# Shorter GpSimd subtractions, more filler products and one moved multiplication in a cluster-attention and mixture-of-experts kernel

## The chip, the core and the metric

The kernel runs on one NeuronCore of a Trainium2 chip, in one launch. Its time is device microseconds. Five engines work side by side, each through its own queue in order: TensorE (PE; its weight loads are listed as PEld), VectorE (DVE), ScalarE (ACT), GpSimd (POOL) and SyncE (SP), which issues most of the DMA transfers.

## The reference

Attention over 16 heads (2 batches of 8), 768 positions, 64 dimensions, is masked by cluster: a query sees a key only where both are nearest to the same of 16 centroids. The result goes through a top-1 mixture of 8 experts with a capacity of 384 rows.

```python
q_assign = argmax(einsum('bhsd,hcd->bhsc', q_n, c_n)); k_assign = ...   # per head
scores = where(q_assign == k_assign, q @ k.T / sqrt(D), -1e9)
attn = softmax(scores);  x = (attn @ v)            # (1536, 512) over all heads
expert_idx = argmax(x @ w_gate); gate_w = its softmax probability
disp[e, pos] = x[i] for the first `capacity` rows of each expert
out[i] = gate_w[i] * (relu(disp[e] @ w1[e]) @ w2[e])[pos]
```

All inputs are fp32.

## The kernel before

**Two-part numbers.** A product on TensorE is made of a rounded high part and the remainder, so that fp32 accuracy is kept. ACT makes the high part by a copy to the fp32r type, and DVE or GpSimd makes the remainder by a subtraction. `split` (line 271) does so for q and k of a head in four steps: step 0 copies q into `W` on ACT and subtracts into `ql` on GpSimd (line 284), step 1 copies k into `Y1` on ACT (line 287), step 2 issues two DMAs, step 3 subtracts into `Y0` on GpSimd (line 293). Each subtraction covers 64 partitions by 768 elements and is followed by a DMA on SP that duplicates a part of it. `split_v` (line 165) does it for v of two heads (128 x 780, line 170), and `p_low` (line 372) for the exponentials of two key tiles (128 x 768, line 376), on DVE except for the eight pairs named in `POOL_PL`, which go to GpSimd.

**A head.** `max_tile` (line 299) multiplies a key block into a 128 x 384 PSUM tile `m`, and DVE takes the row maximum (line 313). The maxima of a head are turned into a row of `Qs`, so that `st_group` (line 354) gets scores with the maximum subtracted: two products (lines 361 and 362), then two exponentials on ACT (line 370). `pv_group` (line 378) multiplies with v in three products (line 387), the third of which needs the remainder `pl`. The loop over 16 heads `i` and 12 groups `g` runs the score products four groups ahead of the value products, and the maxima half a head to a head ahead. `hooks` (line 554) puts the other work at fixed (i, g): the splits of head i+3, the cluster assignment of the pair after next (`cl_scores` line 176, `cl_assign` line 204, `cl_back` line 255), the output (`out_stage`, line 397), and in head 8 the gate, which ends with six scatters by GpSimd (line 527).

**Order.** The prologue is under `tc.manual_schedule()`: each engine's order there is as written. From `warm()` on the Tile framework's planner orders the instructions by its own costs, between `no_sync_barrier` marks before heads 1 and 3 to 8.

**Fillers.** `keep_warm(n, d)` (line 835) issues n products of a constant 128 x 128 tile whose result nobody reads; each shows as two matmul instructions in the trace. In the prologue, `max_tile` is called with `warm=WARM1` (one filler) for four of its six tiles, and `max_part` issues six.

**After the heads** the experts run (`moe`, line 618), TensorE products throughout, with weight loads, ACT copies and DVE subtractions; GpSimd only scatters rows there.

Of the kernel before, what the change touches and what calls it, by code (L numbers as in the profile page):

```python
# [7 lines left out]
F32 = mybir.dt.float32  # L8
# [4 lines left out]
ALU = mybir.AluOpType  # L13
# [3 lines left out]
P = 128  # L17
# [6 lines left out]
def kernel(  # L24
# [140 lines left out]
    def split_v(pi):  # L165
        v = vt[pi]
        hi = work.tile([P, 2, NT, VW + 1], R32, tag="vh", name="vh", bufs=2)
        lo = work.tile([P, 2, NT, VW + 1], R32, tag="vl", name="vl", bufs=2)
        nc.scalar.activation(out=hi[:, :, :, 0:VW], in_=v, func=AF.Copy)
        nc.gpsimd.tensor_tensor(out=lo[:, :, :, 0:VW], in0=v, in1=hi[:, :, :, 0:VW].bitcast(F32), op=ALU.subtract)  # L170
        vt[pi, "h"], vt[pi, "l"] = hi, lo


# [94 lines left out]

    ql = {}

    def split(h, step, eng=nc.gpsimd):
        par = h % 2
        d = pair[h // 2]
        W, Y1, Qs, Y0 = (pick(t, h) for t in (W_t, Y1_t, Qs_t, Y0_t))
        a, c = MAIN[par], PIECE[par]
        p0, p1 = slice(a.start, a.start + 32), slice(a.start + 32, a.stop)

        def dup(dst, src):
            nc.sync.dma_start(out=dst.bitcast(F32), in_=src.bitcast(F32))

        if step == 0:
            nc.scalar.activation(out=W[a], in_=d["q"][a], func=AF.Copy)  # L282
            ql[h] = work.tile([P, S], R32, tag="ql", name="ql", bufs=2)
            eng.tensor_tensor(out=ql[h][a], in0=d["q"][a], in1=W[a].bitcast(F32), op=ALU.subtract)  # L284
            dup(W[c], ql[h][p0])
        elif step == 1:
            nc.scalar.activation(out=Y1[a], in_=d["k"][a], func=AF.Copy)
            dup(Y1[c], Y1[p0])
        elif step == 2:
            dup(Qs[a], W[a])  # L290
            dup(Qs[c], ql.pop(h)[p1])
        elif step == 3:
            nc.gpsimd.tensor_tensor(out=Y0[a], in0=d["k"][a], in1=Y1[a].bitcast(F32), op=ALU.subtract)
            dup(Y0[c], Y1[p1])


# [75 lines left out]
    def p_low(h, g):  # L372
        if g % 2 == 1:
            ph, pl, pf = pt[h, g]
            eng = nc.gpsimd if (h, g) in POOL_PL else nc.vector
            eng.tensor_tensor(out=pl, in0=pf, in1=ph.bitcast(F32), op=ALU.subtract)  # L376

    def pv_group(h, g):
        j, kt = divmod(g, NT)
# [174 lines left out]
    def hooks(i, g):  # L554
        if g in (3, 9) and 2 <= i < 6:
            zero_fill(2 * (i - 2) + g // 6)
        if i == H and g == 5:
            gens["g"] = gate(0)
        if i == H and g >= 5:
            next(gens["g"], None)  # L560
        if i == 3 and g == 0:
            for c in range(4):
                w_load(c)
        if (i, g) in W_AT:
            c = W_AT.index((i, g))
            w_split(c)
            w_load(c + NA)
        if i == 0:
            if g < 4:
                next(gens["c"], None)  # L570
            if g == 4:
                cl_back(1)
            if g in (2, 3, 4, 5):
                split(2, g - 2)

        n = i + 1
        if g == G_CHAIN and n < NH:
            max_chain(n)
        if g == G_ROWS and n < NH:
            max_rows(n)  # L580
        for st in range(4):
            if i + 3 < NH and g == G_SPLIT[st]:
                split(i + 3, st)
        if (i, g) == (H + 1, 1):
            close_tile()
        if (i, g) == (H + 1, 3):
            row0.append(wra.tile([P, XR], F32, tag="z", name="row0", bufs=1))
            nc.sync.dma_start(out=row0[0], in_=xd[0:P, :])
        if (i, g) == (NH - 1, NT + 4):
            out_stage(i, 0, TH)  # L590
        if (i, g) == (NH - 1, NT + 5):
            gens["g"] = gate(B - 1, 0, TH)
            next(gens["g"], None)
        if i >= 1 and g == G_OUT:
            out_stage(i - 1)
        if i % 2 == 1:
            pi = (i + 1) // 2 + 1
            if pi < NH // 2:
                if g in G_SC:
                    n_ = NT // len(G_SC)  # L600
                    cl_scores(pi, 1, G_SC.index(g) * n_, (G_SC.index(g) + 1) * n_)
                if g == G_AS[0]:
                    gens["c"] = cl_assign(pi, AS_MUL)
                for _ in range(G_AS.count(g)):
                    next(gens["c"], None)
            if g == 0 and (i + 1) // 2 + 2 < NH // 2:
                load_pair((i + 1) // 2 + 2)
            if g == 0 and pi < NH // 2:
                load_v(pi)
        else:  # L610
            pi = i // 2
            if g == G_BACK and i > 0 and pi + 1 < NH // 2:
                cl_back(pi + 1)
            if g == G_SV and pi + 1 < NH // 2:
                split_v(pi + 1)
# [258 lines left out]
    def prologue():  # L874
        nc.vector.memset(onef, 1.0)
        nc.vector.memset(nbig, -BIG)
        nc.sync.dma_start(out=cbr, in_=cb)
        load_pair(0, ("q",))
        nc.sync.dma_start(out=cs, in_=cst)
        load_pair(0, ("k",))  # L880
        load_pair(1)
        load_v(0)
        nc.sync.dma_start(out=rhb, in_=rh)
        load_v(1)
        nc.scalar.activation(out=nbig2, in_=onef[:, 0:1], func=AF.Sqrt)
        keep_warm(5, psM.tile([P, 512], F32, tag="m", name="warm"))
        for lst in (W_t, Y1_t, Qs_t, Y0_t):
            zero_rows(lst, 0)
        one_row(0, 0)
        one_row(1, 0)  # L890
        nc.gpsimd.tensor_copy(c16b, cs[:, C_C16:C_C16 + 16])
        for lst in (W_t, Y1_t, Qs_t, Y0_t):
            zero_rows(lst, 1)
        nc.vector.memset(ohb, 0.0)
        nc.vector.memset(oneb, 1.0)

        sq, fps = centroid_scale()
        cl_scores0("q", 0, 3)
        nf = centroid_spread(sq, fps)
        cl_scores0("q", 3, NT)  # L900
        nc.vector.tensor_copy(idb, ident)
        nc.vector.tensor_tensor(out=cbs, in0=cbr, in1=nf, op=ALU.mult)
        aq, ak = (cl_assign(0, nc.vector, nf[:, 0:1], nm) for nm in "qk")
        next(aq)
        split(0, 0, nc.vector)
        cl_scores0("k")
        split(0, 1)
        nc.scalar.activation(out=nbig2, in_=onef[:, 0:1], func=AF.Exp)
        for _ in aq:
            pass  # L910
        for _ in ak:
            pass

        held = work.tile([P, 1], BF16, tag="held", name="held", bufs=1)
        nc.gpsimd.tensor_copy(held, ohb[:, NT - 1, 96:97])
        cl_scores(1, 3, 0, NT // 2)
        tq = psO.tile([64, S], BF16, tag="o", name="ctq")
        tk = psO.tile([64, S], BF16, tag="o", name="ctk")
        cl_back0("q", tq)
        mask0("q", tq, 0, slice(0, S), nc.scalar)  # L920
        cl_scores(1, 3, NT // 2, NT // 2 + 1)
        split(0, 2)
        cl_back0("k", tk)
        mask0("k", tk, 0, slice(0, HALF), nc.vector)
        mask0("k", tk, 0, slice(HALF, S), nc.scalar)
        split(0, 3)
        mask0("q", tq, 1, slice(0, S), nc.scalar)
        mask0("k", tk, 1, slice(0, S), nc.scalar)
        split(1, 0)
        split(1, 1)  # L930
        split(1, 3)
        split(1, 2)
        split_v(0)
        for j in range(2):
            one_row(j, 1)
        for k in range(NT):
            if k in (1, 3):
                t = NT // 2 + 1 + k // 2
                cl_scores(1, 3, t, t + 1)
            max_tile(0, k // 2, k % 2, *((psS, "s") if k % 5 < 3 else (psM, "m")), warm=0 if k in (1, 3) else WARM1)  # L940
        max_part(0, 0)
        gens["c"] = cl_assign(1, nc.vector)
# [13 lines left out]
    with ExitStack():  # L956
        todo = []
        for i in range(NH):
            if i in (1, 3, 4, 5, 6, 7, 8):
                tc.no_sync_barrier()  # L960
            for g in range(2 * NT):
                st_group(i, g)
                todo.append((i, g))
                if i == 0 and g < NT:
                    max_tile(1, g, 0)
                    max_tile(1, g, 1)
                else:
                    n, k = (i + 1, NT + g) if g < NT else (i + 2, g - NT)
                    if n < NH:
                        max_tile(n, k // 2, k % 2)  # L970
                if len(todo) > PLAG:
                    p_low(*todo[-1 - PLAG])
                if len(todo) > LAG:
                    pv_group(*todo.pop(0))
                hooks(i, g)
# [79 lines left out]
```

## Time and profile before

| | |
|---|---|
| median of 3 runs | 515.59 us (511.2 to 516.54) |
| profiled execution | 517.28 us, span of the trace 515.5 us |
| PE, PEld busy | 486.8 us (94%), 420.4 us (82%) |
| DVE busy | 374.7 us (73%) |
| ACT, POOL busy | 318.2 us (62%), 148.1 us (29%) |
| mean granted TensorE clock | 0.976 of full speed |
| chain that ended last | issue 11%, DMA of weights 2%, the rest below 1% each |

The busy time of PE is an upper bound, since pipelined matmuls overlap in the records. The granted clock is given as a share of 2.4 GHz: 1.00 is 2.4 GHz, and 0.50 is 1.2 GHz. Times of rows count from the start of the span. A bracket at the end of a row says how long the engine had been idle before the instruction and what released it.

### The profile page before, as it was taken

The page shows a single profiled execution, that of the slowest core. Times are in us where ns is not written, and L with a number is a line of the kernel's source. Part 1 is how long each engine was busy: PE and PEld are TensorE (multiplying, and loading weights), DVE is VectorE, ACT ScalarE, POOL GpSimd, SP SyncE. Part 2 cuts the span into 40 slices and gives each one's busy share as a digit, 9 for nine tenths or more (in the row PEclk, how much of TensorE's full clock was granted, in tenths as well). Part 3 has the DMA queues.
Part 4 walks back from the last instruction along what each step waited for, and adds up shares of the span by engine and source line. Part 5 has one row for each costly group of instructions (what it writes and reads, how often), then busy time and mean ns, then how long its engine had stood idle before and what let it go on. Part 6 is the DMA issues. An engine that isn't in the chain of part 4 may idle for free. (4 is left out here: it accounts for less than half of the span.)

```text
span 515.5 us, 8317 instructions
## 1 busy us (share of the span) xinstructions
PE 486.8 (94%) x2917; PEld 420.4 (82%) x2917; DVE 374.7 (73%) x650; ACT 318.2 (62%) x642; POOL 148.1 (29%) x122
## 2 busy tenths in 40 slices
PE   8789999989999997899999999999999999999994
PEld 7667988879889886788888866889898989898873
DVE  5796597987997889999988675584757565665411
ACT  3665497687786986878787853464645445373310
POOL 5677144464434545435100040001000000101001
PEclk9888698999999999999999999999999999999999
DMA  7456436777242453431201038676758484855001
GB/s 227 90 135 186 156 81 242 274 238 237 93 116 69 93 197 89 103 89 33 71 2 42 1 125 314 222 252 203 242 205 287 171 294 149 286 170 197 0 9 41
DMA packets 31152, 77.69 MB, mean 151 GB/s; under 512 B 4710, under 2 KB 5056, under 8 KB 31106
## 3 DMA queue, kind: packets, MB, share of 16 engines
q1 hardware_dynamic: 26162, 60.94, 38.6%
q0 software_dynamic: 4944, 16.15, 8.3%
q8 instruction: 27, 0.44, 0.3%
q14 instruction: 19, 0.16, 0.1%
HBM read 50.07 MB, written 17.45 MB: 131 GB/s over the span
## 5 line engine op out<-in xcount | busy, mean ns | idle before, releaser
L370 ACT ACTIVATE pf<-s 128x384 f32<-128x384 f32 x192 | 94.7, 493 | 58.0 <-PE s L362 46.5
L313 DVE TENSOR_REDUCE mx<-m 128x1 f32<-128x384 f32 x192 | 101.6, 547 | 23.6 <-PE m L306 22.2
L376 DVE TENSOR_TENSOR pl<-pf,ph 128x768 fp32r<-128x768 f32 x88 | 100.2, 1138 | 10.7 <-ACT ph L370 8.3
L132 DVE TENSOR_TENSOR ws<-wraw,ws 128x1024 fp32r<-128x1024 f32 x64 | 78.7, 1248 | 26.5 <-ACT ws L126 26.3
L370 ACT ACTIVATE ph<-s 128x384 fp32r<-128x384 f32 x192 | 94.3, 491 | 0.0
L742 PE MATMUL g<-xh,ws 128*128 128x256 f32 x448 | 80.6, 282 | 0.1
L126 ACT ACTIVATE ws<-wraw 128x1024 fp32r<-128x1024 f32 x64 | 66.0, 1052 | 20.8 <-DMA wraw<-in_w_dram 19.6
L674 PE MATMUL g<-ws,hh 128*128 128x512 f32 x240 | 76.5, 400 | 1.6 <-PEq L831 0.7
L306 PE MATMUL m<-Y,W 112*128 112x384 f32 (+1 forms) x192 | 69.7, 370 | 6.9 <-DVE mx L313 6.3
L387 PE MATMUL o<-pl,vh 128*65 128x384 f32 x192 | 66.8, 348 | 5.2 <-DVE pl L376 4.6
L742 PEld LDWEIGHTS g<-xh,ws 128*128 128x128 f32 x448 | 69.6, 190 | 1.1 <-DVE hl L747 0.3
L527 POOL DMA_INDIRECT out_dram<-y,row x17 | 16.5, 972 | 187.3 <-DVE y L667 135.9
L361 PE MATMUL s<-W,Y 112*128 112x384 f32 (+1 forms) x192 | 69.8, 364 | 0.0
L362 PE MATMUL s<-Qs,Y 97*128 97x384 f32 (+1 forms) x192 | 66.3, 350 | 1.1 <-DMA Qs<-mr 1.0
L387 PE MATMUL o<-ph,vh 128*65 128x384 f32 x192 | 66.2, 345 | 0.0
L387 PE MATMUL o<-ph,vl 128*65 128x384 f32 x192 | 66.1, 344 | 0.0
L742 PE MATMUL g<-xl,ws 128*128 128x256 f32 x224 | 63.1, 282 | 0.0
L746 ACT ACTIVATE hh<-g 128x256 fp32r<-128x256 f32 x56 | 21.4, 385 | 60.6 <-PE g L742 58.7
L674 PEld LDWEIGHTS g<-ws,hh 128*128 128x128 f32 x240 | 43.5, 188 | 11.5 <-issue 1.9
L306 PEld LDWEIGHTS m<-Y,W 112*128 112x128 f32 (+1 forms) x192 | 37.9, 198 | 16.2 <-DVE mx L313 14.7
L674 PE MATMUL g<-ws,hl 128*128 128x512 f32 x120 | 47.3, 394 | 0.3 <-DVE hl L647 0.3
L284 POOL TENSOR_TENSOR ql<-qv,W 64x768 fp32r<-64x768 f32 x15 | 29.2, 1947 | 49.3 <-ACT W L282 32.8
(184 smaller groups left out, 779.6 us busy)
## 6 DMA issues: line engine op xcount, KB each, us to landing
wraw<-in_w_dram SPq DMA_DIRECT2D x64, 512.0 KB
row<-xd SPq DMA_DIRECT2D x25, 260.0 KB
xd<-z POOLq DMA_DIRECT2D x7, 780.0 KB, 5.1
v<-in_v_dram SPq DMA_DIRECT2D x8, 390.0 KB
qv<-in_qT_dram SPq DMA_DIRECT2D x8, 384.0 KB
kv<-in_kT_dram SPq DMA_DIRECT2D x8, 384.0 KB
Y<-Y SPq DMA_DIRECT2D x32, 96.0 KB
Qs<-W SPq DMA_DIRECT2D x16, 192.0 KB
```

Source lines behind the costliest of these rows:

```text
L126: nc.scalar.activation(out=w[:, 0], in_=raw[c], func=AF.Copy)
L132: nc.vector.tensor_tensor(out=w[:, 1], in0=t, in1=w[:, 0].bitcast(F32), op=ALU.subtract)
L284: eng.tensor_tensor(out=ql[h][a], in0=d["q"][a], in1=W[a].bitcast(F32), op=ALU.subtract)
L306: nc.tensor.matmul(out=m[:, 0:HALF], lhsT=W[0:KA[h % 2], t * P:(t + 1) * P], rhs=Y1[0:KA[h % 2], j * HALF:(j + 1) * HALF], start=True, sto ...
L313: nc.vector.tensor_reduce(out=mxt[h][:, j, t:t + 1], in_=m[:, 0:HALF], axis=AX.X, op=ALU.max)
L361: nc.tensor.matmul(out=s[:, 0:HALF], lhsT=Y1[0:ka, ks], rhs=W[0:ka, qs], start=True, stop=False)
L362: nc.tensor.matmul(out=s[:, 0:HALF], lhsT=Y0[0:kb, ks], rhs=Qs[0:kb, qs], start=False, stop=True)
L370: nc.scalar.activation(out=o[:, g % 2], in_=s[:, 0:HALF], func=AF.Exp, scale=1.0 / float(D) ** 0.5)
L376: eng.tensor_tensor(out=pl, in0=pf, in1=ph.bitcast(F32), op=ALU.subtract)
L387: nc.tensor.matmul(out=ot[h, j][0:VW, 0:HALF], lhsT=lhs, rhs=r, start=(kt == 0 and n == 0), stop=(kt == NT - 1 and n == 2))
L674: nc.tensor.matmul(out=ps[:, 0:DM], lhsT=h[:, f, ts], rhs=w[:, a, fs], start=(f == 0 and n == 0), stop=(f == KF - 1 and n == 2),)
L742: nc.tensor.matmul(out=ps[:, 0:w_], lhsT=w[:, a, fs], rhs=x[e][:, k, :], start=(n == 0), stop=(n == 3 * KD - 1))
```

## The change

Four edits. The subtractions on GpSimd are issued in pieces: `ql` and `Y0` in thirds of 256 columns, v and the GpSimd share of `pl` in halves. Where the engine is DVE the instruction stays whole. The cluster code multiplication of the pair assigned in head 9 (`i == H + 1`) goes from GpSimd to DVE. In the prologue four filler products are put before the transposes of the k assignment and two behind them. In head 0 the first of the two maximum tiles of each of the groups 0 to 5 gets one filler product ahead of it.

```diff
-        nc.gpsimd.tensor_tensor(out=lo[:, :, :, 0:VW], in0=v, in1=hi[:, :, :, 0:VW].bitcast(F32), op=ALU.subtract)
+        for j in range(2):
+            nc.gpsimd.tensor_tensor(
+                out=lo[:, j, :, 0:VW], in0=v[:, j], in1=hi[:, j, :, 0:VW].bitcast(F32), op=ALU.subtract
+            )
...
+    def minus(eng, out, a, b):
+        n = out.shape[-1]
+        w = n if eng is nc.vector else -(-n // 3)
+        for c in range(0, n, w):
+            cc = slice(c, min(c + w, n))
+            eng.tensor_tensor(out=out[:, cc], in0=a[:, cc], in1=b[:, cc].bitcast(F32), op=ALU.subtract)
...
-            eng.tensor_tensor(out=ql[h][a], in0=d["q"][a], in1=W[a].bitcast(F32), op=ALU.subtract)
+            minus(eng, ql[h][a], d["q"][a], W[a])
...
-            nc.gpsimd.tensor_tensor(out=Y0[a], in0=d["k"][a], in1=Y1[a].bitcast(F32), op=ALU.subtract)
+            minus(nc.gpsimd, Y0[a], d["k"][a], Y1[a])
...
-            eng.tensor_tensor(out=pl, in0=pf, in1=ph.bitcast(F32), op=ALU.subtract)
+            if eng is nc.vector:
+                eng.tensor_tensor(out=pl, in0=pf, in1=ph.bitcast(F32), op=ALU.subtract)
+            else:
+                for j in range(2):
+                    eng.tensor_tensor(out=pl[:, j], in0=pf[:, j], in1=ph[:, j].bitcast(F32), op=ALU.subtract)
...
-                    gens["c"] = cl_assign(pi, AS_MUL)
+                    gens["c"] = cl_assign(pi, nc.vector if i == H + 1 else AS_MUL)
...
         split(0, 2)
+        keep_warm(4, psM.tile([P, 512], F32, tag="m", name="warm"))
         cl_back0("k", tk)
+        keep_warm(2, psM.tile([P, 512], F32, tag="m", name="warm"))
...
                 if i == 0 and g < NT:
-                    max_tile(1, g, 0)
+                    max_tile(1, g, 0, warm=WARM1)
                     max_tile(1, g, 1)
```

## Rows read from the trace of the kernel before

**Rows 1.** Waits of PE, 60 to 290 us: us in total, times, longest.

```profile
PE m L306 <- DVE mx L313: 4.4, 9, 1.3
PE o L387 <- DVE pl L376: 3.0, 1, 3.0
```

**Rows 2.** Windows: three stretches with the TensorE clock at half.

```profile
15.79:19.20 3.41, 3.41 (x17) 3.41 (x16) 2.04 (x4) 3.35 (x5) 1.01 (x2) 0.50 0.03 5
...
46.51:60.16 13.65, 13.65 (x53) 12.45 (x52) 7.93 (x9) 4.85 (x11) 3.48 (x4) 0.50 0.67 224
77.23:80.64 3.41, 3.41 (x12) 2.85 (x11) 3.27 (x8) 1.74 (x4) 2.42 (x2) 0.50 0.22 68
```

**Rows 3.** Groups of DVE instructions by form: busy us, mean ns, idle before.

```profile
L376 DVE TENSOR_TENSOR pl<-pf,ph 128x768 fp32r<-128x768 f32 x88 | 100.2, 1138 | 10.7 <-ACT ph L370 8.3 <-PE o L387 1.9
...
L425 DVE TENSOR_TENSOR lg<-lg,lt 128x48 f32<-128x48 f32 x13 | 9.6, 737 | 0.0
```

**Rows 4.** Timeline of DVE, prologue and head 0: start us, duration us.

```profile
15.84 0.56 DVE L313 TENSOR_REDUCE mx<-m 128x1 f32<-128x384 f32 x1 [0.55 <-PE m L306]
...
20.54 1.69 DVE L326 TENSOR_TENSOR mxp<-mx 128x3 f32<-128x3 f32 x1
...
22.40 1.62 DVE L503 CAST ebr<-cs 1x8 bf16<-1x8 f32 x1
...
29.19 0.20 DVE L326 TENSOR_TENSOR mxp<-mx 128x3 f32<-128x3 f32 x1
```

**Rows 5.** Timeline of POOL, same stretch.

```profile
20.40 1.80 POOL L293 TENSOR_TENSOR Y<-kv,Y 64x768 fp32r<-64x768 f32 x1
22.28 1.72 POOL L170 TENSOR_TENSOR vl<-v,vh 128x780 fp32r<-128x780 f32 x1
...
29.33 3.91 POOL L293 TENSOR_TENSOR Y<-kv,Y 64x768 fp32r<-64x768 f32 x2
```

**Rows 6.** Timeline of PE, same stretch.

```profile
14.17 0.52 PE L243 MATMUL ctk<-idb,ohb 128*64 128x128 bf16 x6 [0.98 <-DVE ohb L233]
...
19.68 1.50 PE L838 MATMUL mtd<-onef 128*128 128x128 f32 x12
22.28 0.49 PE L332 MATMUL mtd<-cs,mxp 128*1 128x128 f32 x3 [1.09 <-DVE mxp L326]
...
25.00 0.44 PE L306 MATMUL m<-Y,W 112*128 112x384 f32 x1 [1.21 <-DVE mx L313]
```

**Rows 7.** Timeline of DVE: subtractions, and one multiplication, beside GpSimd's or alone.

```profile
31.21 0.35 DVE L225 TENSOR_TENSOR ceq<-ceq,c16b 128x384 bf16<-128x384 bf16 x1
...
38.70 0.94 DVE L376 TENSOR_TENSOR pl<-pf,ph 128x768 fp32r<-128x768 f32 x1
...
46.10 3.22 DVE L376 TENSOR_TENSOR pl<-pf,ph 128x768 fp32r<-128x768 f32 x1
...
70.03 1.80 DVE L376 TENSOR_TENSOR pl<-pf,ph 128x768 fp32r<-128x768 f32 x1
...
194.43 3.91 DVE L376 TENSOR_TENSOR pl<-pf,ph 128x768 fp32r<-128x768 f32 x1
```

**Rows 8.** Timeline of POOL in heads 1 and 9.

```profile
69.16 1.85 POOL L284 TENSOR_TENSOR ql<-qv,W 64x768 fp32r<-64x768 f32 x1 [2.41 <-PE s L361]
70.97 2.56 POOL L293 TENSOR_TENSOR Y<-kv,Y 64x768 fp32r<-64x768 f32 x1
...
193.89 1.87 POOL L284 TENSOR_TENSOR ql<-qv,W 64x768 fp32r<-64x768 f32 x1
195.68 1.83 POOL L293 TENSOR_TENSOR Y<-kv,Y 64x768 fp32r<-64x768 f32 x1
```

**Rows 9.** Timeline of ACT: the copies that the two `Y0` subtractions wait for.

```profile
69.95 0.84 ACT L287 ACTIVATE Y<-kv 64x768 fp32r<-64x768 f32 x1
...
188.08 0.83 ACT L287 ACTIVATE Y<-kv 64x768 fp32r<-64x768 f32 x1
```

**Rows 10.** Waits of SP's own DMA queue: us in total, times, longest.

```profile
SPq L347 <- ACT mr L346: 54.6, 7, 12.7
```

## The prediction

> **What bounds the kernel now.** I read the page first: TensorE is busy nearly throughout and has the largest sum, so time is won where it stands idle or runs slowly. The waits of PE come second. From 60 to 290 us, where the heads run, almost all of its idle time ends at DVE: 4.4 us in 9 waits for a maximum, and 3.0 us in one wait for a subtraction [rows 1]. Third, the windows: the granted clock is 0.50, which is 1.2 GHz instead of 2.4, in stretches of 3.41, 13.65 and 3.41 us [rows 2]; each begins just after a time in which PE had stood idle or done little. At half speed a stretch in which PE is always busy costs up to half its length.
>
> Fourth, why DVE is late. The groups by form show it: the subtraction of 128x768 has a mean of 1138 ns over 88, but one with GpSimd idle takes 0.94 us, so 88 x 0.198 = 17.4 us go in excess; the addition of 48 elements a row has a mean of 737 ns over 13 [rows 3, 7]. The timelines of DVE and POOL, laid side by side, give the cause. A maximum of two 128x3 pieces takes 0.20 us alone and 1.69 us when it starts at 20.54, and it ends at 22.23, where GpSimd's subtraction of 20.40 ends (22.20); a cast of eight elements takes 1.62 us and ends at 24.02, with GpSimd's of 22.28 (24.00) [rows 4, 5]. So a DVE instruction that reads two tiles from SBUF, or casts there, stands until GpSimd's running subtraction is over. The row maxima, which read PSUM, are not slowed.
>
> **The parts and their cost.** The sum is made against the profiled execution's own 517.28 us (a span of 515.5 and 1.8 around it); the median shown, 515.59, is 1.7 lower.
>
> *Pieces: what they cost GpSimd.* ql and Y0 of 15 and 16 heads become thirds, v of 8 pairs and 8 pl become halves: 30 + 32 + 8 + 8 = 78 more instructions. Between neighbours the trace has +0.08 us (20.40 + 1.80 against 22.28) [rows 5] to -0.04 us (69.16 + 1.85 against 70.97) [rows 8], so -3 to +6 us of GpSimd's time in all, at most 0.16 for one split. Its cover is that GpSimd works for a head up to three later. What is queued behind it is on SP: the duplicate of ql waits for GpSimd, and behind that stands the DMA that carries the maxima to the scores. But SP stands 54.6 us waiting for ACT to hand it that row [rows 10], so 0.16 us drowns, and so does one DVE instruction of 0.94 that slips in between pieces. I take 0; with the cover gone it is 0.16 a head, 2.6.
>
> *Pieces: does DVE get in?* In head 1 it did, between ql and Y0: the subtraction that starts at 70.03 took 1.80, while Y0 took 2.56 instead of 1.83 [rows 7, 8]. At 31.21 a multiplication of two SBUF tiles took 0.35 in the middle of two Y0 that follow each other from 29.33 to 33.24 [rows 5, 7]. In head 9 it did not: the one of 194.43 waited through ql and Y0, 3.91 us [rows 7, 8], and one of 3.22 at 46.10 looks alike [rows 7]. I take the first, by the row at 31.21, where GpSimd's second instruction had nothing left to wait for, as a second piece has. The Trainium skill, GPSIMD Engine Reference, "Instruction dispatch", speaks for the other: each of GpSimd's cores begins the next instruction as soon as its own share of the last is done, so that no end of a piece would be free. By the rows taken the sum is 509.0, by that rule it is the first rival's 515.6.
>
> *Pieces: what they give.* If DVE gets in, a wait that now averages half an instruction becomes half of a third or of a half, and GpSimd's cluster multiplications stay whole; I take 40% as what is left. Of PE's 4.4 us of waits for maxima between 60 and 290 [rows 1] that saves 60%, 2.6 (0 to 4.4).
>
> *Head 9.* After the scatters GpSimd does ql and Y0 back to back from 193.89 to 197.5, and DVE's subtraction of 194.43 takes 3.91 instead of 0.94 [rows 7, 8]; that is PE's wait of 3.0 us [rows 1]. A third of 1.87 is 0.62, so DVE starts at 194.5 or 195.1 and ends by 196.1. Of 3.0 I count 2.5 (0 to 3.0).
>
> *The moved multiplication.* GpSimd's queue loses it behind ql and Y0 of head 9, with nothing urgent in line behind it. DVE gains one of 0.35, the time of the same form at 31.21 [rows 7]. It sits among tiles whose result is needed a head later: 0 (-0.35 to +0.35).
>
> *Prologue.* PE waits 0.98 us for the k assignment before its transposes [rows 6]. Twelve filler instructions take 1.50 us, 0.125 each, and a product is two, so four products fill 1.0 us of that and the two behind the transposes 0.5 us, of which about half lies in a wait for the mask. Cost 0 to 0.3. What they aim at is the stretch from 15.79 at half clock [rows 2]. If it stays at 1.00, the six maxima run at DVE's pace, six times 0.56 from 15.84 [rows 4], and end near 19.2 instead of 20.5: 1.3 earlier at most, I take 1.0. Then the small maximum waits for a piece of 0.6 at most, 0.3 in the mean, where it lost 1.69 - 0.20 = 1.49 [rows 4]; PE's transposes waited for it (1.09 idle) [rows 6]. Together 1.0 + 1.2, less the overrun: 2.0 (-0.3 to 2.8).
>
> *Head 0.* The cast of 22.40 would wait for half of 1.72, so it ends some 0.7 earlier [rows 4, 5]; DVE's next maximum ended a wait of PE of 1.21 us [rows 6]. I count 0.7. The six fillers cost 6 x 0.25 = 1.5 us of PE. DVE takes 0.56 us for a maximum [rows 4] and there are two buffers, so most of it hides in waits for DVE; if that cover is gone all 1.5 shows. I take 0.3. Net 0.4 (-1.5 to 1.2).
>
> *The clock later.* The stretch from 77.23 [rows 2] follows a wait of PE for a maximum that was behind a blocked subtraction. If the wait shrinks the stretch may not come, worth 3.41/2 = 1.7; I count half, 0.8 (0 to 1.7). The long one from 46.51 follows six maxima in a row that no edit touches, so I leave it where it is: 0 in the sum.
>
> The sum: 2.6 + 2.5 + 0 + 2.0 + 0.4 + 0.8 = 8.3, so 517.28 - 8.3 = 509.0 us. The low and high ends of the terms give 519 and 504.
>
> **Rivals.**
>
> *GpSimd keeps its hold across pieces: 515.6.* What sets head 9 apart from head 1 in the rows is when Y0 was free to go. In head 9 ACT's copy was done at 188.91, long before ql began; in head 1 at 70.79, in the middle of ql [rows 9]. Pieces two and three never wait for anything, so they are like head 9; against it stands only the row at 31.21. Then the pieces give nothing. The prologue keeps 2.0, since the small maximum now comes before Y0 of 20.40 has begun and may get in there as in head 1; head 0 costs its 0.3: 517.28 - 1.7 = 515.6.
>
> *The long slow stretch goes: 502.* The stretch of 13.65 us costs 6.8 [rows 2]. With PE's work shifted by 2 us and filled, it may not begin. 509.0 - 6.8 = 502.2. For it: the runs shown lie between 511.2 and 516.54, a spread that one such stretch would make. Against: the run of maxima ahead of it is untouched.
>
> *It grows: 522, slower.* Place: the end of head 0 and head 1. The fillers sit in the first half of head 0 and leave less for PE to do at its end, when DVE takes the maxima one by one; the clock then falls as now, and stays down through head 2 as well, for another 13.65 us, 6.8. With the hold kept as in the first rival: 515.6 + 6.8 = 522.4. It decides if the granted clock is not back at 1.00 soon after 60 us. Against: the stretch of before ended at 60.16 with the same products to come, and the fillers add to PE's work.
>
> **How the numbers follow.** The forecast has 53%, the held port 27%, the lost stretch 10%, the grown one 10%. The predicted time is 509. About 1% (5.2 us) is what a measurement can tell from no change here: below 510.4 is faster, above 520.7 slower. Four fifths of the forecast's chance (42%), the lost stretch (10%) and a tenth of the held port (3%) are faster: 55%. The grown stretch is slower: 10%. The rest, 35%, is the same. The range reaches from the lost stretch, 501, to the held port with the six fillers at their full 1.5 us and some spread of the runs, 518.
>
> **What would show it.** Right: DVE's 128x768 subtraction falls from a mean of 1138 ns to about 1020, the addition from 737 to about 400; PE's waits for maxima between the prologue and 290 us to about 2 us, and no wait of 3 us after the scatters; no 0.50 near 16 us. Wrong: DVE instructions that still end where the last piece of a subtraction ends; a mean above 1100; a new stretch at 0.50 of ten or more us; PE waiting in head 0 for its own fillers, seen as maxima of DVE that wait for PE.

## The result, and the profile after

The changed kernel takes 507.09 us (median of 21 runs, 502.93 to 514.76), the kernel before in the same session 514.06 us (21 runs, 510.22 to 517.96). The ratio is 0.985, with an interval of 0.982 to 0.988: faster by 1.5%, and 1.9 us under the forecast of 509.0. A ratio is taken over the faster runs of either kernel alone (those within 1.5% of its fastest, here 12 of the changed kernel's 21), so it holds few of the long stretches at half clock that come next.

The runs of the changed kernel lie in two groups by their mean granted clock: 11 at 0.982 and above take 502.9 to 507.1 us, 10 at 0.976 and below take 510.4 to 514.8, and the profiled execution (514.46 us, span 512.7) is one of the latter. The windows of it show why: the columns are the stretch, its length, the busy time of PE, PEld, DVE, ACT and POOL with the number of instructions, then the granted clock, the DMA share and GB/s.

```profile
17.00:20.40 3.40, 3.40 (x27) 3.40 (x27) 2.70 (x6) 2.68 (x4) 0.67 (x1) 1.00 0.02 5
44.53:61.59 17.06, 16.98 (x59) 14.38 (x60) 8.76 (x14) 6.97 (x15) 8.86 (x14) 0.50 0.68 229
194.72:198.13 3.41, 3.34 (x12) 2.24 (x11) 3.11 (x5) 2.31 (x6) 1.95 (x2) 0.50 0.61 165
```

Against [rows 2], the stretch at half clock near 16 us is gone and so is the one at 77, but the long one has stayed and is 17 us. A second profile of the same kernel (e3 below, span 504.9) has none at 0.50 from 14.2 to 502 us. Where I count what the change did, I use that one.

The groups of DVE's instructions by form, which answer to [rows 3]:

```profile
L388 DVE TENSOR_TENSOR pl<-pf,ph 128x768 fp32r<-128x768 f32 x88 | 95.2, 1081 | 11.3 <-ACT ph L381 9.8 <-PE o L402 0.9
...
L440 DVE TENSOR_TENSOR lg<-lg,lt 128x48 f32<-128x48 f32 x13 | 4.8, 373 | 0.0
```

The small addition fell from 737 to 373 ns, the subtraction only from 1138 to 1081. The waits of PE from 60 to 290 us, which answer to [rows 1] (us in total, times, longest):

```profile
PE m L317 <- DVE mx L324: 3.9, 7, 2.2
PE s L373 <- DMA Qs<-mr: 1.4, 1, 1.4
```

The wait of 3.0 us for a subtraction is gone, but of the 3.9 us for maxima one wait alone has 2.2, and that is in head 9, just where the 3.0 had been. And from 0 to 62 us there are two waits that are new (for GpSimd's `pl` PE waited 0.5 us before, for the scaling not at all):

```profile
PE o L402 <- POOL pl L391: 3.1, 1, 3.1
PE fps L878 <- DVE csq L872: 1.9, 1, 1.9
```

**The first, in the prologue.** Timelines of DVE, POOL and PE of the changed kernel at 5 us (start, duration, and in brackets the idle time before):

```profile
5.25 2.75 DVE L872 TENSOR_SCALAR csq<-cs,css 128x128 f32<-128x128 f32 x1
5.45 2.61 DVE L916 CAST idb<-cs 128x128 bf16<-128x128 f32 x1
```

```profile
5.15 0.73 POOL L884 MEMSET W<- 32x768 f32 x1
5.83 0.73 POOL L884 MEMSET Y<- 32x768 f32 x1
6.51 0.73 POOL L884 MEMSET Qs<- 32x768 f32 x1
7.19 0.73 POOL L884 MEMSET Y<- 32x768 f32 x1
```

```profile
8.05 0.58 PE L878 MATMUL fps<-csq,onef 128*128 128x128 f32 x1 [1.91 <-DVE csq L872]
```

A scaling of 128x128 on DVE, 0.95 us before, takes 2.75 and ends at 8.00, behind GpSimd's four clears (7.19 + 0.73 = 7.92).

**The second, at the end of head 0.** First POOL before, then POOL and PE after:

```profile
25.66 3.71 POOL L284 TENSOR_TENSOR ql<-qv,W 64x768 fp32r<-64x768 f32 x2
...
33.31 2.31 POOL L170 TENSOR_TENSOR vl<-v,vh 128x780 fp32r<-128x780 f32 x1
39.59 3.75 POOL L376 TENSOR_TENSOR pl<-pf,ph 128x768 fp32r<-128x768 f32 x2 [3.96 <-ACT ph L370]
```

```profile
28.78 5.33 POOL L280 TENSOR_TENSOR ql<-qv,W 64x256 fp32r<-64x256 f32 x6
34.07 5.65 POOL L280 TENSOR_TENSOR Y<-kv,Y 64x256 fp32r<-64x256 f32 x6
39.79 1.83 POOL L171 TENSOR_TENSOR vl<-v,vh 128x390 fp32r<-128x390 f32 x2
41.59 3.88 POOL L391 TENSOR_TENSOR pl<-pf,ph 128x384 fp32r<-128x384 f32 x4
```

```profile
42.63 0.39 PE L402 MATMUL o<-pl,vh 128*65 128x384 f32 x1 [3.08 <-POOL pl L391]
```

Before, the four subtractions and that of v took 25.66 to 35.62, 9.96 us, and GpSimd then idled 3.96 us for its first `pl`. Now the same work begins 3.1 us later and takes 28.78 to 41.62, 12.84 us: the pieces themselves cost some time (three thirds take 2.12 us with DVE away, as at 191.77 below, one whole 1.83), and DVE slips in between them. The slack is gone and PE waits 3.08 us for the first `pl`.

**Head 9**, behind the scatters: DVE, POOL and PE after, which answer to the last row of [rows 7], to [rows 8] and to the second of [rows 1].

```profile
192.70 0.56 DVE L324 TENSOR_REDUCE mx<-m 128x1 f32<-128x384 f32 x1 [3.06 <-remote]
...
194.57 1.52 DVE L388 TENSOR_TENSOR pl<-pf,ph 128x768 fp32r<-128x768 f32 x1
```

```profile
190.79 0.98 POOL L542 DMA_INDIRECT xd<-x,gsi  x1 [0.30 <-issue]
191.77 2.12 POOL L280 TENSOR_TENSOR ql<-qv,W 64x256 fp32r<-64x256 f32 x3
193.83 2.85 POOL L280 TENSOR_TENSOR Y<-kv,Y 64x256 fp32r<-64x256 f32 x3
```

```profile
193.31 0.44 PE L317 MATMUL m<-Y,W 112*128 112x384 f32 x1 [2.24 <-DVE mx L324]
```

The subtraction fell from 3.91 to 1.52 us, as forecast. But ahead of it DVE now stands 3.06 us before a maximum, released by something that the profile doesn't name ("remote"), and PE waits 2.24 us for that. Of the fourteen profiles seven have this standstill (changed, e1 to e4, e6, e7) and seven do not.

**All profiles by stretch.** Worked out from the traces, in us: the start of head 0 is the first product of line 372 (361 before), a head goes from its first such product to that of the next, heads 10 to 15 end where the last value product starts, the rest is what is left of the span. A star marks stretches that hold 3.4 us or more at 0.50 (in the last column but one the end of the span is left out, where all fall).

```
              start   head 0  head 1  2 to 8  head 9  10 to 15  rest   span
before        22.96*  22.47*  23.30*  117.50* 20.41   90.53     218.3  515.5
changed       22.44   24.22   23.67*  113.75  21.21*  89.13     218.3  512.7
e1            19.51   23.67*  17.00   113.67  20.78*  88.28     219.0  501.9
e2            19.59   24.04*  17.00   116.10  21.02*  90.55     218.1  506.3
e3 (changed)  22.62   23.76   16.98   113.70  20.31   89.13     218.4  504.9
e4            22.69   23.90   16.75   113.75  20.30   89.15     217.5  504.1
e5            19.05   23.94*  16.74   113.89  21.52*  89.02     218.2  502.4
e6            20.37   23.91   16.70   111.42  20.26   89.15     218.0  499.8
e7            21.26*  23.48*  16.86   113.81  20.98*  89.12     217.7  503.2
e8            21.33   24.19   17.00   113.79  18.96   89.12     217.9  502.3
e9            18.55   23.86   16.71   111.56  21.69*  88.97     217.9  499.2
e10           19.53   26.13*  16.73   111.53  19.35   88.28     217.9  499.5
e11           19.48   25.39*  17.00   116.01* 21.94*  90.56     218.1  508.5
e12           22.57   23.74   17.01   113.78  19.37   88.24     217.9  502.6
```

### The profile page after: what moved, and what is told of

Same layout as the page of the kernel before. It is cut to its first block, busy times and chain, and to the rows that moved or that the text cites. A ratio compares the mean times of both kernels' runs of the same rounds, so it can differ in the third digit from the quotient of the medians.

```text
span 512.7 us, 8439 instructions
## 1 busy us (share of the span) xinstructions
PE 487.0 (95%) x2941; PEld 423.0 (83%) x2941; DVE 364.4 (71%) x651; ACT 318.1 (62%) x642; POOL 167.2 (33%) x199
## 5 line engine op out<-in xcount | busy, mean ns | idle before, releaser
L388 DVE TENSOR_TENSOR pl<-pf,ph 128x768 fp32r<-128x768 f32 x88 | 95.2, 1081 | 11.3 <-ACT ph L381 9.8
L132 DVE TENSOR_TENSOR ws<-wraw,ws 128x1024 fp32r<-128x1024 f32 x64 | 77.3, 1227 | 26.2 <-ACT ws L126 26.1
L317 PE MATMUL m<-Y,W 112*128 112x384 f32 (+1 forms) x192 | 68.2, 365 | 4.2 <-DVE mx L324 3.9
L280 POOL TENSOR_TENSOR ql<-qv,W 64x256 fp32r<-64x256 f32 x45 | 38.1, 875 | 43.7 <-ACT W L293 22.7
```

What stands on the lines that cost most here:

```text
L132: nc.vector.tensor_tensor(out=w[:, 1], in0=t, in1=w[:, 0].bitcast(F32), op=ALU.subtract)
L280: eng.tensor_tensor(out=out[:, cc], in0=a[:, cc], in1=b[:, cc].bitcast(F32), op=ALU.subtract)
L317: nc.tensor.matmul(out=m[:, 0:HALF], lhsT=W[0:KA[h % 2], t * P:(t + 1) * P], rhs=Y1[0:KA[h % 2], j * HALF:(j + 1) * HALF], start=True, sto ...
```

## The experiments

Four kernels ran on one chip each time, beside the kernel before; a ratio is always to the kernel before of the same session (511.96, 513.37 and 514.65 us in the three).

**e1, the pieces alone.** The kernel before with the subtractions in thirds and halves; no filler of the change, the multiplication on GpSimd.

> The kernel before with the pieces alone (no new filler products, multiplication back on GpSimd). Port theory (a DVE instruction gets in at the end of a piece, and this is most of the gain): DVE's 128x768 subtraction has a mean near 1080 ns instead of 1138, the addition near 320 instead of 737, and the time is 3 to 5 us below the kernel before. Clock theory (most of the gain is that fewer of the stretches at half clock come): the same means, but a time within 2 us of the kernel before.

Measured: 505.58 us (503.21 to 511.52), ratio 0.989 (0.985 to 0.993). The addition is at 386 ns, `pl` at 1089. The pieces alone give what the whole change gives, and GpSimd does not keep its hold across pieces in general. Outside head 9 the largest single wait that they end is one of PE for a maximum in head 10, behind a subtraction of weights on DVE. DVE, POOL and PE of e2 (subtractions whole), then DVE and POOL of e1:

```profile
201.22 2.40 DVE L132 TENSOR_TENSOR ws<-wraw,ws 128x1024 fp32r<-128x1024 f32 x1
```

```profile
199.97 2.56 POOL L293 TENSOR_TENSOR Y<-kv,Y 64x768 fp32r<-64x768 f32 x1
```

```profile
204.14 0.44 PE L306 MATMUL m<-Y,W 128*128 128x384 f32 x1 [1.25 <-DVE mx L313]
```

```profile
197.71 1.30 DVE L132 TENSOR_TENSOR ws<-wraw,ws 128x1024 fp32r<-128x1024 f32 x1
```

```profile
197.89 3.80 POOL L280 TENSOR_TENSOR Y<-kv,Y 64x256 fp32r<-64x256 f32 x3
```

In e1 PE has no such wait there.

**e2, the fillers alone**, in the prologue and in head 0.

> The kernel before with the fillers alone, those of the prologue and those of head 0. Port theory: within 2 us of the kernel before, since DVE waits as before (mean 1138 ns). Clock theory: no stretch at half clock before 30 us, and a time 3 to 6 us below the kernel before; in runs in which the stretch after head 0 is missing the mean clock is above 0.985 and the time is 5 to 8 us lower than in the others.

Measured: 511.50 us (508.12 to 513.32), ratio 1.001 (0.998 to 1.003): nothing. The addition stays at 707 ns; the mean of `pl` is 1094 with the subtractions whole, so that mean is a poor witness for the pieces. In the table, e1 and e2 differ where the pieces act: heads 2 to 8 by 2.4 us, heads 10 to 15 by 2.3. In both stretches PE has the same products in the same order in the two traces, 699 and 545, so another order by the planner is not what they gain by.

**e3, the changed kernel again.**

> The changed kernel once more, for its spread and another trace. Both theories: about 7 us below the kernel before in the median. Clock theory: its runs fall into two groups some 8 us apart, those with a mean clock near 0.975 and those near 0.99, and a trace of the second kind has no stretch of ten or more us at half clock between 40 and 65 us. Port theory alone: one group, with the same clock in all runs.

Measured: 511.73 us (504.06 to 516.87, 7 runs), ratio 0.988 (0.982 to 0.993). Three runs with a mean clock of 0.994 or more take 504 to 506.7 us, four at 0.975 or less 511.7 to 516.9. The trace has both new waits, 2.75 us for the scaling and 3.08 us of PE for `pl`: they belong to the kernel, the long stretch at half clock belongs to some of its executions.

**e4, fillers at the end of head 0 as well**, two before each of the last six maximum tiles of the run that precedes the long stretch.

```diff
-                        max_tile(n, k // 2, k % 2)
+                        max_tile(n, k // 2, k % 2, warm=2 if i == 0 else 0)
```

> The changed kernel, and two filler products ahead of each of the six maximum tiles of head 2 that are taken in the second half of head 0, where PE waits for DVE. Clock theory: the stretch at half clock after head 0 no longer comes in any run, the mean clock is above 0.985 in all, and the median is near 504 us, 3 below the changed kernel. Port theory: PE does 3 us of empty work, the time is the same or up to 3 us longer.

Measured: 503.05 us (500.89 to 506.11), ratio 0.985 (0.981 to 0.990). The same stretch as in the first window above:

```profile
44.50:61.60 17.10, 17.10 (x115) 15.57 (x114) 14.28 (x26) 11.45 (x28) 13.48 (x19) 1.00 0.77 260
```

115 matmul instructions and 1.00 where the changed kernel had 59 and 0.50. All kernels with these fillers (e4, e5, e6, e7, e9, e10) ran 34 times, with a mean clock of 0.986 or more each time; kernels with pieces but without them (changed, e1, e3, e8, e12) ran 57 times, 21 of these at 0.978 or less. So fillers at that place keep the long stretch away, and those of the change stood too early for it. That points to the thin work of PE at the end of head 0 as what sets it off; the profiled execution of e3 had the same thin work and no such stretch.

**e5, GpSimd's clears later.** e4 with the four clears of the second buffers' rows moved from the start of the prologue to where GpSimd idles.

```diff
         nc.gpsimd.tensor_copy(c16b, cs[:, C_C16:C_C16 + 16])
-        for lst in (W_t, Y1_t, Qs_t, Y0_t):
-            zero_rows(lst, 1)
...
+        for lst in (W_t, Y1_t, Qs_t, Y0_t):
+            zero_rows(lst, 1)
         split(1, 0)
```

> The kernel of e4 with GpSimd's four clears of the second buffers' rows (32x768, 0.73 us each at 5.15 to 7.9 us) moved behind the prologue's splits, to about 17.7 us, where GpSimd is idle for 3 us. Theory A (GpSimd keeps DVE out over a row of back-to-back instructions): csq, 2.75 us on DVE in every trace that has both the pieces and the fillers, takes under 0.4 us and PE's wait of 1.8 us for it goes; head 0's first score product comes at 20 to 21 us instead of 22.7, and the time falls by 1.5 to 2.5 us, to a ratio of 0.980 to 0.983 against the kernel before where e4 had 0.985. Theory B (the 2.75 us is DVE's own, a clock or a late operand): csq stays over 2 us and nothing moves. Theory C (hidden): csq is short, but head 0 starts no earlier, since the max tiles' chain ahead of it ends on something else; ratio 0.985.

Measured: 501.70 us (501.40 to 504.16), ratio 0.979 (0.973 to 0.986). DVE at 5 us, in the timeline of e5:

```profile
5.25 0.28 DVE L872 TENSOR_SCALAR csq<-cs,css 128x128 f32<-128x128 f32 x1
5.45 0.22 DVE L914 CAST idb<-cs 128x128 bf16<-128x128 f32 x1
```

0.28 where e4 has 2.87: theory A for the scaling. By the time alone e4 and e5 can't be told apart, since their intervals overlap. Head 0 starts at 19.05 instead of 22.69, 3.6 us earlier where the wait was 1.8. The rest goes by the clock that PE has behind the wait. The same twelve products of the prologue, in the timelines of PE of e3 and of e6 (which also has the wait, of 1.94 us):

```profile
9.92 2.77 PE L199 MATMUL ctp<-cbr,kv 128*128 128x128 f32 x12
```

```profile
9.06 1.50 PE L199 MATMUL ctp<-cbr,kv 128*128 128x128 f32 x12
```

At nearly twice the duration they run at half clock in e3, as does what follows until the profile's first record of a granted clock at 14.2 us; in e6 that record is at 6.3, and its head 0 starts at 20.37. In e7, where PE waits 2.67 us for the scaling, until 8.05, the record begins early enough to show the clock itself:

```profile
7.84:11.25 3.41, 3.20 (x15) 3.20 (x16) 1.57 (x6) 2.35 (x4) 0.07 (x1) 0.50 0.89 293
```

Of e5's 3.6 us head 9 gave 1.2 back in the profiled execution. There DVE, POOL and PE have:

```profile
187.19 2.54 DVE L330 TENSOR_TENSOR mxx<-mx 128x6 f32<-128x6 f32 x1
```

```profile
187.76 1.95 POOL L391 TENSOR_TENSOR pl<-pf,ph 128x384 fp32r<-128x384 f32 x2
```

```profile
190.77 0.69 PE L317 MATMUL m<-Y,W 128*128 128x384 f32 x1 [2.33 <-DVE mx L324]
```

A maximum of two 128x6 pieces, 0.15 us at its shortest, takes 2.54 and ends at 189.73. It starts in the last third of a `Y0`, which ends at 187.79, and stands until both halves of a `pl` are over (189.71). PE waits 2.33 us for a row maximum queued behind it, and in that wait a stretch of 3.4 us at half clock begins. So here pieces kept DVE out over three ends, with no DMA issue of GpSimd near: the last one before it began at 180.30.

**e6, the zero fills on SP's queue**, on e4.

```diff
-            nc.gpsimd.dma_start(out=v, in_=ztile[0][:, :, 0:w].to_broadcast([P, v.shape[1], w]))
+            nc.sync.dma_start(out=v, in_=ztile[0][:, :, 0:w].to_broadcast([P, v.shape[1], w]))
```

> The kernel of e4 with the zero fills (16 issues in heads 2 to 5) sent from SP's queue instead of GpSimd's. Theory A (a subtraction of DVE is kept out longest right behind GpSimd's DMA issues, whose work puts the instructions behind them close together): the three subtractions on DVE of 1.7 to 2.6 us at about 90, 107 and 125 us fall to 1.45 us or less, the time by 1 to 2 us, a ratio of 0.982 to 0.983 where e4 had 0.985. Theory B (those three are only places where two subtractions of GpSimd meet one of DVE): they stay, or come back at other places with the same excess, and the time stays within 0.3%. The scatters of head 9 stay on GpSimd, and the subtraction behind them is to be as in e4 in either case.

Measured: 500.52 us (500.22 to 502.60), ratio 0.978 (0.971 to 0.985). The same place in head 5, first POOL and DVE of e4, then of e6:

```profile
99.07 0.59 POOL L564 DMA_DIRECT2D out_dram<-z  x1
99.67 2.13 POOL L280 TENSOR_TENSOR Y<-kv,Y 64x256 fp32r<-64x256 f32 x3
101.76 0.77 POOL L564 DMA_DIRECT2D xd<-z  x1
```

```profile
100.02 2.61 DVE L388 TENSOR_TENSOR pl<-pf,ph 128x768 fp32r<-128x768 f32 x1 [0.41 <-ACT ph L381]
```

```profile
93.76 2.17 POOL L280 TENSOR_TENSOR ql<-qv,W 64x256 fp32r<-64x256 f32 x3 [3.38 <-issue]
95.88 2.85 POOL L280 TENSOR_TENSOR Y<-kv,Y 64x256 fp32r<-64x256 f32 x3
```

```profile
96.06 1.39 DVE L388 TENSOR_TENSOR pl<-pf,ph 128x768 fp32r<-128x768 f32 x1 [1.20 <-ACT ph L381]
```

In e4 three thirds right behind a DMA issue take 2.13 us, with nothing between them, and DVE's subtraction, which arrives in the first, waits for all three. In e6 the thirds take 2.85, because DVE got in after the first, and DVE's takes 1.39. The three subtractions of 1.7 to 2.6 us that e4 has near 84, 100 and 118 us are gone; no `pl` takes over 1.5, the mean falls to 1048 ns, heads 2 to 8 from 113.75 to 111.42 us. Theory A holds for the subtractions. For the time it is not shown: the intervals of e4 and e6 overlap, and of the 2.33 us in these heads 1.42 is a wait of PE in e4 that lies ahead of the 2.61 us subtraction, for the DMA that carries the maxima to the scores:

```profile
97.87 0.44 PE L373 MATMUL s<-Qs,Y 97*128 97x384 f32 x1 [1.42 <-DMA Qs<-mr]
```

In e6 PE has no such wait. 26 of its 699 products there also stand at other places in PE's order.

**e7, no `pl` of head 0 on GpSimd**, on e4: (0, 7) and (0, 9) taken out of `POOL_PL`.

> The kernel of e4 with the two subtractions of pl in head 0 (groups 7 and 9) on DVE instead of GpSimd. Theory A (head 0 ends late because GpSimd's queue, stretched by its splits, reaches these two last): PE's wait for GpSimd's pl (3.1 us in the second run of the changed kernel, 0.3 us in e4) is gone, head 0 is 1 to 3 us shorter than 23.8 us, the time falls by 1 to 2 us. Theory B (DVE is the bound at the end of head 0, with six max tiles to reduce): DVE takes 1.9 to 2.5 us more there, the max tiles of head 1 come later, head 0 gets longer by 1 to 2 us, and the time rises by as much.

Measured: 501.34 us (499.78 to 504.99), ratio 0.979 (0.972 to 0.985). The wait for GpSimd's `pl` is gone and head 0 is 0.4 us shorter than in e4 in spite of 3.4 us at half clock; theory B is out (it had head 0 longer by 1 to 2 us). How much of the time it is can't be said: e4's wait was only 0.3 us, and the intervals of e4 and e7 overlap.

**e8, without the fillers of head 0**, on the changed kernel.

> The changed kernel without its filler products in head 0 (those of the prologue stay). Theory A (the fillers of head 0 are what keeps the clock up there): a stretch at half clock is back near 46 us in most runs, and the time goes to 511 to 515 us. Theory B (they do nothing for the clock and cost PE about nothing): the same as the changed kernel, a ratio of 0.985 to 0.989 against the kernel before. Theory C (they delay the max tiles of head 1): head 0 is shorter by 0.3 to 0.5 us, ratio 0.984 to 0.987.

Measured: 506.75 us (501.57 to 514.50, 11 runs), ratio 0.985 (0.981 to 0.990). The same as the changed kernel, with the same two groups of runs (4 of 11 at 0.978 or less): theory B. The fillers of head 0 neither bring nor prevent the long stretch.

**e9, the three edits together** (e4, e5 and e6).

> The changed kernel with three edits together: the late fillers of e4, GpSimd's clears moved as in e5, the zero fills on SP's queue as in e6. Theory A (the edits act at three places, 5 to 8 us, 45 to 62 us and 90 to 130 us, and add): csq under 0.4 us, no subtraction of pl over 1.6 us but perhaps the one behind the scatters, head 0 from 19 us on; a span 2 us under the 499.8 us of e6, a time of 498 to 500 us, a ratio of 0.973 to 0.977. Theory B (what one edit gives, the next wait takes): 500 to 502 us, a ratio of 0.978.

Measured: 500.06 us (499.56 to 501.02), ratio 0.971 (0.969 to 0.974). The scaling takes 0.28 us, no `pl` over 1.5, and head 0 starts at 18.55: the three edits act at their places as theory A had it. The ratio is lower than theory A's, but the kernel before was 1.3 us slower beside e9 than beside e6; in us the median is 0.5 under e6's, so that the gains add is not shown by the time. The profiled span is 0.6 us under e6's, not 2: head 9 took 1.4 us more. It has what e5 has there, a maximum of 128x6 that takes 2.54 us over pieces of GpSimd, a wait of PE of 2.34 for it and 3.4 us at half clock, though the zero fills are on SP here.

**e10, e9 with nothing left of the change but the pieces.**

> The kernel of e9 without the fillers of the change (prologue and head 0) and with the multiplication on GpSimd again: of the change only the pieces are left. Theory A (the pieces are the change's whole gain, as e1, e2 and e8 say): the same time as e9 within 0.3%. Theory B (the fillers of the change carry the clock through the prologue and head 0): a stretch of 3.4 us at half clock near 20 to 26 us, as in e1 and e2, costing 1.0 to 1.7 us, and in some runs more; 0.3% or more slower than e9.

Measured: 500.28 us (498.58 to 501.55), ratio 0.971 (0.968 to 0.974), the same as e9. But not because the fillers do nothing here. The same stretch, first in e10, then in e9:

```profile
23.13:29.95 6.82, 6.53 (x20) 5.56 (x21) 3.59 (x8) 4.70 (x10) 6.57 (x9) 0.50 0.62 180
```

```profile
23.13:29.95 6.82, 6.25 (x42) 5.31 (x41) 6.42 (x13) 5.25 (x12) 6.57 (x9) 1.00 0.48 146
```

e10 reaches the end of head 0 at 45.66 us, e9 at 42.42: in these two executions 3.2 us for the fillers, with the stretch that theory B named. From head 9 to 15 it is the other way, 107.6 against 110.7 us. There the two kernels differ by the moved multiplication alone. 0.7 of the 3.0 us lies in heads 10 to 15, where e12 shows the same by itself; 2.3 lies in head 9, with the late maximum and the half clock of e9.

**e11, the kernel before with the zero fills on SP.**

> The kernel before with the zero fills on SP's queue, and nothing else: GpSimd's subtractions stay whole. Theory A (behind its DMA issues GpSimd keeps DVE out over two instructions, whole or in pieces): the long subtractions of pl of the kernel before in heads 2 to 5 fall to 1.7 us or less, the mean of pl by 20 to 40 ns, the time by 1 to 2 us, a ratio of 0.996 to 0.998. Theory B (only small pieces have a gap that the issues can take away): no subtraction changes by more than its phase, a ratio of 0.999 to 1.001.

Measured: 513.11 us (509.27 to 518.22), ratio 0.995 (0.991 to 0.998). The group and a long subtraction in head 3, with POOL beside it:

```profile
L376 DVE TENSOR_TENSOR pl<-pf,ph 128x768 fp32r<-128x768 f32 x88 | 102.1, 1160 | 11.3 <-ACT ph L370 9.5 <-PE o L387 1.2
```

```profile
80.50 2.50 DVE L376 TENSOR_TENSOR pl<-pf,ph 128x768 fp32r<-128x768 f32 x1 [0.17 <-ACT ph L370]
```

```profile
80.36 1.82 POOL L293 TENSOR_TENSOR Y<-kv,Y 64x768 fp32r<-64x768 f32 x1
```

Theory A's mechanism is out: the mean did not fall, and subtractions of 2.3 to 2.5 us remain without any DMA issue ahead, since a whole `Y0` is 1.8 us long. The time is 0.5% less all the same. The sum for heads 2 to 8 is as in e2 and hides where: heads 2 to 5 take 65.28 us against 67.09, and head 6 takes 17.63 against 15.90, with a stretch at half clock that e2 doesn't have:

```profile
135.47:138.88 3.41, 3.41 (x14) 2.95 (x13) 2.42 (x7) 1.03 (x3) 1.72 (x1) 0.50 0.25 60
```

PE's wait for the DMA with the maxima (0.96 us in e2) is gone here as it is in e6. So in these executions the move of the fills brings 1.8 us in these heads with whole subtractions too, and most of what e6 gained does not need the pieces. Whether it is the wait, the other order of PE's products (26 of 699, as in e6) or something else was not taken apart.

**e12, the multiplication back on GpSimd**, on the changed kernel.

> The changed kernel with the one multiplication of head 9 on GpSimd again, as before the change. My sum put its move at nothing. Theory A (it was hidden on either engine): head 9 stays between 19 and 21.2 us, the time within 0.3% of the changed kernel's ratio of 0.985 to 0.9875. Theory B (on GpSimd it makes the subtraction of pl behind it wait, as its 1.57 us would do): head 9 is 0.5 to 1.5 us longer and a pl near 190 us takes 2 us or more.

Measured: 502.96 us (500.79 to 511.45), ratio 0.975 (0.972 to 0.979): 1% better than the changed kernel's 0.985 to 0.988, which neither theory had. About half of that is the kernel before, which was 2.7 us slower beside e12 than beside e3; the runs with a mean clock of 0.982 or more average 502.6 us against 505.0 in e3. Against e3 the stretches are the same up to head 9 (within 0.1 us each). Head 9 is 0.94 us shorter and heads 10 to 15 are 0.89 shorter. But head 9 of e3 has the standstill of DVE, and e8, with the move and without the standstill, has 18.96 us against e12's 19.37. So only the 0.89 is put to the move by the profiles. In head 9 of e12 DVE waits for GpSimd's product:

```profile
192.13 0.55 DVE L231 TENSOR_REDUCE cm<-ceq 128x24 bf16<-128x384 bf16 x1 [2.13 <-POOL ceq L228]
```

## Why the prediction was right, and which of its steps were not

The time, 507.09, is 1.9 us from the forecast. The mechanism that carried it holds: DVE gets in between pieces, e1 shows it alone, and the rival that GpSimd keeps its hold across pieces (515.6) is refuted as the general case. But the terms of the sum of 8.3 were off in both directions, and that the total came so near is luck. The sum was made for an execution in which the long stretch at half clock stays. By their clock, the ten runs that have it take 510.4 to 514.8 us, the eleven without it 502.9 to 507.1. The forecast of 509.0 lies between the groups, and the median, 507.09, is the slowest run of the eleven; in e3 the median fell into the other group, 511.73. The sum also started from an execution of the kernel before that was 3.2 us above its median of 514.06, and between the medians the gain is 7.0 us and not 8.3.

**Pieces, outside head 9: 2.6 forecast, 4.7 measured.** e2 against e1: heads 2 to 8 116.10 to 113.67, heads 10 to 15 90.55 to 88.28. The step took 60% of PE's idle time for maxima [rows 1], and that share is right: outside head 9 those waits fall from 4.3 us in e2 to 1.5 in e1. What it left out is time in which PE is not idle by the records: over the 1244 products, the same in the same order, PE is busy 2.2 us less in e1. So the bound of 4.4 was exceeded. Why the products take less is not shown.

**What pieces cost GpSimd: 0 forecast, with a bound of 0.16 a split; 0.3 a split, and it is not covered in head 0.** Three thirds without DVE between them take 2.12 to 2.17 us against 1.81 to 1.83 whole. With DVE between them they take 2.85. The step named the right cover, GpSimd's lead, and looked only at what SP fetches from it; its 2.6 us for a lost cover is not in the sum's low end of 519 either. The `pl` of group 7 in head 0 is queued behind the splits on GpSimd itself, with 3.96 us of slack before, and PE waits 3.08 us for it.

**Head 9: 2.5 forecast, 0.1 measured** (20.41 to 20.31 in e3). The subtraction got out as forecast, 3.91 to 1.52 us. What was late next was not asked: a standstill of 3.1 us on DVE in front of a maximum, which ends 0.9 to 1.0 us after the last scatter (191.77 to 192.70). It is in e1 (pieces alone) and e2 (fillers alone) too, so it needs neither of them; it is not in the kernel before, nor in e5 and e8 to e12. e8 and e12, without it and without another long wait of DVE for GpSimd's pieces, have 18.96 and 19.37 us, 1.0 to 1.5 less than before: that much of the 2.5 the shorter subtraction can give. What releases DVE in the standstill is not settled.

**The moved multiplication: 0 forecast, a loss of 0.9 us measured** (heads 10 to 15, e3 against e12; the 0.94 us of head 9 go with the standstill). The step priced the instruction on both queues, and 0.35 us on DVE is right. It left out that the planner orders PE's products by all engines' loads: with the move, five products of 545 pass from heads 10 to 12 into head 13, and the same 545 take 89.13 instead of 88.24 us, with PE idle 0.2 us in either. Every profile with the move has 88.97 to 89.15 there, every one with pieces and without it 88.24 to 88.28. That the order is the cause is what is left, not shown by itself.

**Prologue: 2.0 forecast, 0.3 measured** (22.96 to 22.62). The stretch at 0.50 near 16 us went as forecast. In its place came 2.75 us for the scaling at 5.25, PE's wait of 1.9 for it and in e3 half the clock behind that until 14 us. The scaling is so slow in all seven profiles with pieces and prologue fillers whose clears stood there (changed, e3, e4, e6, e7, e8, e12) and in none of the four with at most one of them (before, e1, e2, e11); e5 shows that the clears cause it, and why only those seven meet it is open. The step also rested on one execution: e11 differs from the kernel before in the zero fills alone, the first of which the kernel before issues at 44.11 us, and its head 0 starts at 19.48, 3.5 us before that of the profile that I read. In e2 the fillers alone gain nothing over that.

**Head 0: a gain of 0.4 forecast, a loss of 1.3 in e3.** The step looked at the cast of 1.62 us and not at GpSimd's queue, and in e3 PE waits 3.08 us for `pl`. That wait alone is not the limit: e4, with 0.3 us of it and more fillers, has 23.90 us, and there PE waits 1.3 us for a DMA instead. The end of head 0 moved from 45.43 to 46.38; with e5's clears it is at 42.99.

**The clock later: 0.8 forecast, about 1.4 measured.** The stretch at 77 us is in none of the other thirteen profiles, and heads 2 to 8 take 116.10 in e2 against 117.50. Since e2 has no pieces, its going is not their doing, as the step had it.

**The long stretch: 0 in the sum, 10% for its going.** By the clock of the runs it went in 11 of the 21 and stayed in 10, so forecast and rival each hold a part of the median. The step said that no edit touches the six maxima ahead of it, and e8 bears that out: the fillers of head 0 change nothing. Its growing by 13.65 us (522) did not happen; it grew from 13.65 to 17.06 in the profiled execution.

The Trainium skill, GPSIMD Engine Reference, "Instruction dispatch", has each of GpSimd's cores start the next instruction as soon as its own share of the last is done; the prediction took that to leave no end of a piece free. In the traces that is the exception: behind a zero fill's issue three thirds keep DVE out (2.61 us in e4), in head 9 of e5 and e9 a third and two halves do (2.54), and elsewhere DVE mostly waits for the end of one piece.

## What to carry to other kernels

Shortening what blocks an engine pays over all the places where it blocks, not only at the waits that the profile lists; but look at the longer queue of the engine that is cut up, whose last customer may be the bound's own operand. An edit priced at nothing by its duration can still reorder a planned program, so it has to be run alone: here the one that was to cost nothing cost 0.9 us, and the fillers by themselves brought nothing in the time. Fillers held the clock here where they stood directly ahead of the stretch that falls, which the windows of the profile show, and one profiled execution does not tell which stretches fall in all of them. A sum over several heads can hide a gain behind a stretch at half clock, as in e11, so compare head by head.

The best kernels here are e9 and e10 at 0.971, both faster than the changed one. e9 with the multiplication on GpSimd was not run; by the stretches of e9 (up to head 8) and e10 (from head 9) its span would be some 496 us, an estimate.

## What the hardware showed that I had not expected

- GpSimd's pieces mostly let DVE in at their ends, but not always: 2.61 us for a subtraction of 0.94 over three pieces behind a DMA issue in e4 (1.39 us in e6, where the issues were elsewhere), and 2.54 us for a maximum of 0.15 over three pieces in e5 and e9 with no such issue near. What sets these apart is open.
- Clears, which read nothing, also keep DVE out, over four instructions: 2.75 us for a scaling of 0.28 (in four other profiles it got in behind the first, 0.74 to 0.95 us). The Trainium skill, SBUF — State Buffer, "Who interferes with whom", has the scaling among the operations that can contend with GpSimd, and gives the pair of ports to whoever issues first for the whole instruction. The trace agrees on the contention; the hold, though, lasted for four instructions, not one.
- The same instructions reached head 0 at 22.96 us in one execution (before) and at 19.48 in another (e11).
